# Values of the memory tokens with stationary weights, and another order of the first phase, in a two-part kernel that keeps TensorE busy

## The chip, the cores and the metric

The kernel runs on one core of one Trainium2 chip. The metric is device time in microseconds of one execution. Runs of this kernel agree within half a microsecond, so a difference of about 0.2% (2.5 us) can be told from no change.

The engines are named as the profile names them: PE is TensorE (PEld its weight loads), DVE is VectorE, ACT is ScalarE, POOL is GpSimd, and SP is SyncE, which here only issues DMAs. Each engine takes its instructions in order: one that waits holds up everything behind it on the same engine.

## The reference

Two independent computations on inputs of 2048 tokens with 1024 features, their results side by side:

```python
# Part A: a diagonal state space layer, states complex
dt = jnp.exp(log_dt); Lam_bar = jnp.exp(dt * Lam)
Bu = jnp.einsum('bld,pd->blp', x + 0j, B_bar)
for t in range(L):
    h = Lam_bar[None, :] * h + Bu[:, t, :]
y = 2.0 * jnp.einsum('blp,dp->bld', hseq, Cmat).real + x * Dskip
# Part B: attention in 64 segments of 32 tokens, 8 memory tokens in front of each, 32 heads of 128
for s in range(n_seg):
    h = jnp.concatenate([mem, xs], axis=1)
    q, k, v = (einsum('btd,dhe->bhte', h, W) for W in (Wq, Wk, Wv))
    p = _softmax(where(mask, q @ k * scale, -1e9))
    o = einsum('bhte,hed->btd', p @ v, Wo)
    mem = o[:, :M, :]          # the next segment's memory
    outs.append(o[:, M:, :])
out = jnp.concatenate([a, b], axis=-1)
```

## The kernel before

Part B's recurrence from segment to segment is replaced by a guess of the memory tokens that a last step compares with what comes out. The guess needs 73 columns (`NM`) for the memory tokens that are not ordinary tokens; they stand as columns 2048 to 2120 of `xe`, the transposed input, and are called `memT`.

**First phase (0 to 347 us).** PE alternates between two kinds of work. `values()` computes part B's values: `v_pair` makes two tiles of 128 tokens by 512 value columns, each by eight matmuls of 512 moving columns (`v_mm`, L411) into a PSUM buffer psP or psS (two of each, used in turn), ACT copies each tile to SBUF (L75, buffer `b_vst`), and `v_st` (L419) stores a pair to DRAM by SP's queue. The first eight pairs go to eight buffers of their own (`a_hs` in the profile); from the ninth pair on there are two `b_vst` buffers, so a pair's first copy needs the store of the pair two before to have landed. `stage1(pc, tb)` does part A: 32 times (8 blocks of states by 4 blocks of 512 tokens) 16 matmuls of 512 columns (L256) into psO (two buffers), then on DVE two products with the rotation table from psO (L263, L264), a difference and a sum in fp32 (L266, L267) and two scans along time (L270, L271). `post` then turns the scanned sums back: ACT rounds them to bf16 (`a_g`, one buffer, L288), and DVE makes two products and a sum (L290 to L292). `tables(pc)` makes the next block's rotation tables on DVE and ACT once in four stages. Three or four value tiles stand between two stages, and `og` (L468, 64 moving columns) now and then.

In the first phase the order in which instructions stand on an engine is the tile framework's, except where `keep_in_program_order` pins an instruction to where the program has it. Pinned are the matmuls of the beginning, the scans, all of `post`, the loads of part A's transposed input (`load_x`, `xT`, a transposing DMA of 1 MB each), the loads of Wv from head block 2 on, and the stores `v_st` of the beginning. `post` of stage n-1 is called half way through the value tiles that follow stage n.

**Second phase (347 to 465 us).** `stage2` multiplies the states by C (L310), `guess` makes the guessed memory.

**Attention (465 to 1017 us).** `proj` makes q and k of two heads at a time (L570, eight matmuls of 480 columns a group, and L553), `attention` does eleven units of scores, mask and values for each pair of heads (L596, L599, L603, L614, L619, L621). Values come from DRAM: `load_v(hp)` (L585, L586) reads a pair of heads from `vx` and `vt`. For each of the eight head blocks `v_mem(hb)` makes the values of the 73 memory columns: it loads Wv (1 MB, L403), takes `memT` as the stationary operand and 512 value columns of Wv as the moving one (L502, eight matmuls), copies 73 rows by 512 on ACT, and stores the rows by two DMAs (L505 into `vx`, L506 into `vt`). `v_mem(0)` stands behind nine groups of `proj`, `v_mem(hp + 1)` at unit 4 of pair hp.

**Output (1017 us to the end).** `op` multiplies by Wo (L670), `check` compares the guess (L715: 256 matmuls of 73 moving columns).

Of the kernel before, what the change touches and what calls it, by code (L numbers as in the profile page):

```python
# [9 lines left out]
BF16 = mybir.dt.bfloat16  # L10
I32 = mybir.dt.int32
ACT = mybir.ActivationFunctionType
ALU = mybir.AluOpType
# [13 lines left out]
HB = 8; HP = 16  # L27
# [7 lines left out]
NMX = 7  # L35
NM = NTL + NMX
# [97 lines left out]
class PartA:  # L134
# [92 lines left out]
    def load_x(self, tb):  # L227
        k = self.k
        self.xT[tb] = k.w8((KC, TB), "xT")
        k.tc.keep_in_program_order(  # L230
            k.SP.dma_start(self.xT[tb], self.x[0][tb * TB:(tb + 1) * TB, :], transpose=True))

    def load_b(self, pc):
        k = self.k
# [12 lines left out]
    def stage1(self, pc, tb):  # L247
        k = self.k; V, PE = k.V, k.PE
        pin = k.tc.keep_in_program_order
        if tb == 0:  # L250
            self.carry = None
        cs, rot, ed = self.tabs
        u = k.ps("O")
        for i in range(2):
            for c in range(KC):
                m = PE.matmul(u[:, i, :], self.bt[:, i, c, :], self.xT[tb][:, c, :], start=(c == 0), stop=(c == KC - 1))  # L256
                if self.pin:
                    pin(m)
        c_ = cs[:, 0, 0:TB].unsqueeze(1).to_broadcast([128, 2, TB])
        s_ = cs[:, 1, 0:TB].unsqueeze(1).to_broadcast([128, 2, TB])  # L260
        a = self.wp.tile([128, 2, TB], FP32, name="a_a")
        b = self.wp.tile([128, 2, TB], FP32, name="a_b", bufs=1)
        V.tensor_tensor(a[:], u[:], c_, ALU.mult)  # L263
        V.tensor_tensor(b[:], u[:], s_, ALU.mult)  # L264
        wr, wi = a[:, 0, :], a[:, 1, :]
        V.tensor_tensor(wi, wi, b[:, 0, :], ALU.subtract)  # L266
        V.tensor_tensor(wr, wr, b[:, 1, :], ALU.add)  # L267
        rb = self.rr[:, pc:pc + 1].to_broadcast([128, TB])
        ini = self.carry
        pin(V.tensor_tensor_scan(wr, rb, wr, 0.0 if ini is None else ini[:, 0:1], ALU.mult, ALU.add))  # L270
        pin(V.tensor_tensor_scan(wi, rb, wi, 0.0 if ini is None else ini[:, 1:2], ALU.mult, ALU.add))  # L271
        if tb < NB - 1:
            nx = self.wp.tile([128, 2], FP32, name="a_nx"); tt = self.wp.tile([128, 2], FP32, name="a_tt")
            V.tensor_scalar(tt[:], ed[:, 0:2], wi[:, TB - 1:TB], None, ALU.mult)
            V.scalar_tensor_tensor(nx[:], ed[:, 2:4], wr[:, TB - 1:TB], tt[:], ALU.mult, ALU.add)
            self.carry = nx
        if tb not in self.hs:
            self.hs[tb] = self.hsp.tile([128, PC, 2, TB], BF16, name="a_hs", bufs=4)
        self.prev, self.last = self.last, [a, rot, self.hs[tb][:, pc, :, :]]

    def post(self, last):
        if last is None:
            return
        k = self.k; V = k.V
        pin = k.tc.keep_in_program_order
        a, rot, hp = last
        g = self.wp.tile([128, 2, TB], BF16, name="a_g", bufs=1)
        pin(k.S.activation(g[:], a[:], ACT.Copy))  # L288
        n = self.wp.tile([128, 2, TB], BF16, name="a_n", bufs=1)
        pin(V.tensor_tensor(hp, g[:, 0:1, :].to_broadcast([128, 2, TB]), rot[:, 0:2, :], ALU.mult))  # L290
        pin(V.tensor_tensor(n[:], g[:, 1:2, :].to_broadcast([128, 2, TB]), rot[:, 1:3, :], ALU.mult))
        pin(V.tensor_tensor(hp, hp, n[:], ALU.add))  # L292

    def stage2(self, pool, dB):

# [21 lines left out]
class PartB:  # L317
    def __init__(self, k, x, mem0, Wq, Wk, Wv, Wo, out):
        self.k = k
        self.x, self.mem0, self.out = x, mem0, out  # L320
        self.Wf = [w.rearrange("(c p) h e -> p c (h e)", p=128) for w in (Wq, Wk, Wv)]
        self.Wo = Wo.rearrange("h e d -> e h d")
        self.vx = [k.drp.tile([NSLOT, 512], BF16, name=f"b_vx{i}") for i in range(HB)]
        self.vt = [k.drp.tile([NTL, 512], BF16, name=f"b_vt{i}") for i in range(HB)]
        self.os = [k.drp.tile([T, 1024], BF16, name=f"b_os{i}") for i in range(4)]
        self.omd = k.drp.tile([MT, H * E], BF16, name="b_omd")
        self.od = k.drp.tile([128, H * L], BF16, name="f_od")
        c = k.cst
        self.m0T = c.tile([128, KC, M], BF16, name="b_m0T")
        self.gm = c.tile([128, KC, NM], FP32, name="b_gm")  # L330
        self.xbar = c.tile([128, KC, NSEG], BF16, name="b_xbar")
        self.ogT = c.tile([128, H, NSEG], BF16, name="b_ogT")
        self.accE = c.tile([128, HP * NU], FP32, name="b_accE")
        self.rall = c.tile([128, HP * NU * 4], FP32, name="b_rall")
        self.flag = c.tile([1, 1], I32, name="b_flag")
# [62 lines left out]
    def load_wv(self, hb, w=None, parts=1, e=None, js=None):  # L398
        if w is None:
            w = self.k.w8((KC, 512), "wv")  # L400
        n = KC // parts
        for i in js or range(parts):
            d = (e or self.k.SP).dma_start(w[:, i * n:(i + 1) * n, :], self.Wf[2][:, i * n:(i + 1) * n, hb * 512:(hb + 1) * 512])  # L403
            if self.pin and hb > 1:
                self.k.tc.keep_in_program_order(d)
        return w


# [6 lines left out]
    def v_st(self, hb, q, st, e):  # L415
        vx = self.vx[hb]
        s0 = GX + 2 * q * 128
        n = 2 if q < 7 else 1
        d = e.dma_start(vx[s0:s0 + n * 128, :].rearrange("(i p) n -> p i n", p=128), st[:, 0:n, :])  # L419
        if self.pin:  # L420
            self.k.tc.keep_in_program_order(d)
        if q == 7:
            e.dma_start(vx[0:64, :], st[0:64, 1, :])
            e.dma_start(vx[T - 32:T + 32, :], st[64:128, 1, :])
# [70 lines left out]


    def v_mem(self, hb):
        k = self.k
        w = self.load_wv(hb)
        p = k.ps("P")  # L500
        for c in range(KC):
            k.PE.matmul(p[0:NM, :], self.memT[:, c, :], w[:, c, :], start=(c == 0), stop=(c == KC - 1))  # L502
        st = self.p3.tile([NM, 512], BF16, name="b_vmst", bufs=2)
        k.copy("s", st[:], p[0:NM, :])
        k.SP.dma_start(self.vx[hb][64:64 + NMX, :], st[0:NMX, :])  # L505
        k.SP.dma_start(self.vt[hb][:], st[NMX:NM, :])  # L506


    def qk_init(self, pool):
        V, G = self.k.V, self.k.G  # L510
        self.qk = []
        for i in range(2):
            pair = []
            for n in "qk":
                t = pool.tile([128, 2, QW], BF16, name=f"b_{n}{i}", bufs=1)
                V.memset(t[:, :, 64 + NMX:GX], 0.0)
                V.memset(t[:, :, 21 * GW + 64:21 * GW + GX], 0.0)
                V.memset(t[:, :, NG * GW:QW], 0.0)
                pair.append(t)
            self.qk.append(pair)  # L520
        self.vb, self.mb = [], []
        for i in range(2):
            t = pool.tile([GW, NG, VW], BF16, name=f"b_v{i}", bufs=1)
            G.memset(t[:, :, 0:1], 1.0)
            G.memset(t[:, :, VW - 1:VW], 1.0)
            self.vb.append(t)
        for i in range(4):
            t = pool.tile([GW, 4 * GW + 32], BF16, name=f"b_m{i}", bufs=1)
            G.memset(t[:, 4 * GW:4 * GW + 32], 0.0)
            self.mb.append(t)  # L530
# [315 lines left out]
def kernel_main(tc, A_x, A_Lre, A_Lim, A_Bre, A_Bim, A_Cre, A_Cim, A_logdt, A_Dskip, B_x, B_mem0, B_Wq, B_Wk, B_Wv, B_Wo, out,  # L846
                force=False, dbg=None):
    with ExitStack() as ctx:
        k = K(tc, ctx)
# [3 lines left out]
        a = PartA(k, A_x, A_Lre, A_Lim, A_Bre, A_Bim, A_Cre, A_Cim, A_logdt, A_Dskip, out)  # L853
        b = PartB(k, B_x, B_mem0, B_Wq, B_Wk, B_Wv, B_Wo, out)
# [10 lines left out]
        with pool("p1", "right") as p1:  # L865
# [54 lines left out]
            for n in range(PC * NB):  # L920
# [5 lines left out]
                if tb == 1 and pc + 1 < PC:  # L926
                    nbt = a.load_b(pc + 1)
                want = 20 + 4 * (n + 1) if n < 4 else 36 + (92 * (n - 3) + 27) // 28
                half = done + 2
                while done < want:  # L930
                    next(v, None); done += 1
                    if done == half:
                        a.post(a.prev)
                while done >= 32 and oged < done // 16:
                    b.og(oged, wvs.pop(oged))
                    oged += 1
# [15 lines left out]
                    a.load_c(0, 0)  # L952
                if n == 29:
                    a.load_c(0, 1)
            a.post(a.last)
            k.V.memset(b.rall[:], 0.0)
            a.load_c(1, 0)
            a.load_c(1, 1)
# [20 lines left out]
        with pool("p3", "right") as p3:  # L979
            b.p3 = p3  # L980
            b.qk_init(p3)
            pr, at = b.proj(), b.attention()
            for _ in range(9):
                next(pr)
            b.v_mem(0)
            for _ in range(9):
                next(pr)
            done = 18
            b.wo0, b.acc = [], {}
            early = b.op_some([(0, 0), (1, 0)], range(3), "P")  # L990
            for n, (hp, u) in enumerate(at):
                if u == 4 and hp < 7:
                    b.v_mem(hp + 1)
                if u == 4 and 8 <= hp < 12:
                    w = k.w8((8, 512), "wo0")
                    k.SP.dma_start(w, b.Wo[:, 8 * (hp - 8):8 * (hp - 7), 0:512])
# [113 lines left out]
```

## Time and profile before

| | |
|---|---|
| median of three runs | 1250.3 us (1250.12 to 1250.6) |
| the profiled execution, its own time | 1250.12 us |
| its span in the profile | 1248.4 us, so 1.7 us lie around it |
| PE busy | 1236.3 us, 99% of the span |
| DVE, ACT, POOL busy | 609.4, 329.3, 199.5 us |
| mean granted TensorE clock | 0.998 |

A row of the timeline gives start, duration, engine, line, operation, tiles and, in brackets, the engine's idle time before it and what ended that. Matmuls are pipelined, so a matmul's duration (379 ns for 512 columns) is longer than the time until the next one starts; what a group of matmuls costs is read from where the next group starts.

### The profile page before, as it was taken

The page shows a single profiled execution, that of the slowest core. Times are in us where ns is not written, and L with a number is a line of the kernel's source. Part 1 is how long each engine was busy: PE and PEld are TensorE (multiplying, and loading weights), DVE is VectorE, ACT ScalarE, POOL GpSimd, SP SyncE. Part 2 cuts the span into 40 slices and gives each one's busy share as a digit, 9 for nine tenths or more (in the row PEclk, how much of TensorE's full clock was granted, in tenths as well). Part 3 has the DMA queues.
Part 4 walks back from the last instruction along what each step waited for, and adds up shares of the span by engine and source line. Part 5 has one row for each costly group of instructions (what it writes and reads, how often), then busy time and mean ns, then how long its engine had stood idle before and what let it go on. Part 6 is the DMA issues. An engine that isn't in the chain of part 4 may idle for free. (4 is left out here: it accounts for less than half of the span.)

```text
span 1248.4 us, 19205 instructions
## 1 busy us (share of the span) xinstructions
PE 1236.3 (99%) x7852; PEld 651.9 (52%) x7923; DVE 609.4 (49%) x1117; ACT 329.3 (26%) x757; POOL 199.5 (16%) x284
## 2 busy tenths in 40 slices
PE   9999999999999999999999999999999999999998
PEld 4444444444455445555555655555556554454443
DVE  4889999999931122444444444444444450011000
ACT  4444434444210002323333333333233320000000
POOL 2000000000032130222222222322232230000000
PEclk9999999999999999999999999999999999999999
DMA  9932232333666557576767544645575469606000
GB/s 238 261 109 68 89 98 71 91 93 85 151 213 201 138 163 139 96 141 141 142 122 156 114 122 94 129 82 94 105 139 105 72 195 217 159 18 152 17 26 19
DMA packets 296995, 151.81 MB, mean 122 GB/s; under 512 B 138440, under 2 KB 290240, under 8 KB 296904
## 3 DMA queue, kind: packets, MB, share of 16 engines
q1 hardware_dynamic: 295640, 149.11, 51.9%
q8 instruction: 63, 1.03, 0.4%
q10 hardware_dynamic: 1264, 1.44, 0.4%
q14 instruction: 28, 0.23, 0.1%
HBM read 73.70 MB, written 43.66 MB: 94 GB/s over the span
## 5 line engine op out<-in xcount | busy, mean ns | idle before, releaser
L570 PE MATMUL psP<-b_xe,w 128*128 128x480 bf16 x2048 | 439.7, 366 | 0.0
L570 PEld LDWEIGHTS <-w 128*128 128x128 bf16 x2048 | 194.2, 98 | 185.2
L603 POOL TENSOR_TENSOR b_m<-b_e,maskB 99x396 bf16<-99x396 bf16 x160 | 139.2, 871 | 356.3 <-ACT b_e L599 356.3
L77 DVE CAST b_q<-psP 128x480 bf16<-128x480 f32 (+1 forms) x192 | 98.2, 533 | 150.9 <-PE psP L570 139.4
L411 PEld LDWEIGHTS <-b_xe 128*128 128x128 bf16 x1024 | 99.9, 98 | 120.4 <-ACT b_xe L75 0.6
L670 PEld LDWEIGHTS <-b_ol 128*128 128x128 bf16 x1024 | 99.5, 98 | 117.5
L75 ACT ACTIVATE b_k<-psP 128x480 bf16<-128x480 f32 x128 | 73.1, 571 | 314.3 <-PE psP L570 314.3
L599 ACT ACTIVATE b_e<-psS 99x396 bf16<-99x396 f32 x176 | 87.4, 496 | 173.8 <-PE psS L596 166.6
L621 DVE TENSOR_TENSOR b_ot<-psO,b_rall 99x512 bf16<-99x512 f32 x176 | 121.7, 692 | 6.4
L256 PE MATMUL psO<-w,a_bt 128*128 128x512 bf16 x496 | 114.8, 379 | 0.8
L670 PE MATMUL psS<-w,b_ol 128*128 128x512 bf16 x438 | 99.0, 379 | 0.6
L619 DVE RECIPROCAL b_rall<-psO 99x4 f32<-99x4 f32 x176 | 31.2, 177 | 136.3 <-PE psO L614 136.2
L411 PE MATMUL psS<-w,b_xe 128*128 128x512 bf16 x378 | 90.1, 379 | 0.4
L411 PE MATMUL psP<-w,b_xe 128*128 128x512 bf16 x376 | 89.8, 379 | 0.4
L256 PEld LDWEIGHTS <-a_bt 128*128 128x128 bf16 x512 | 49.7, 98 | 59.0
L310 PEld LDWEIGHTS <-a_hs 128*128 128x128 bf16 x512 | 49.5, 98 | 58.3
L614 PE MATMUL psO<-b_v,b_m 99*128 99x129 bf16 x704 | 70.5, 221 | 0.1
L77 DVE CAST b_ost<-psS 128x512 bf16<-128x512 f32 x13 | 9.0, 692 | 125.4 <-PE psS L670 112.3
L596 PEld LDWEIGHTS <-b_k 128*128 128x128 bf16 x704 | 49.8, 98 | 33.4 <-issue 0.5
L596 PE MATMUL psS<-b_q,b_k 128*128 128x99 bf16 x704 | 60.1, 208 | 0.2
L75 ACT ACTIVATE b_vst<-psS 128x512 bf16<-128x512 f32 x56 | 33.4, 597 | 98.1 <-PE psS L411 70.2
L310 PE MATMUL psS<-w,a_hs 128*128 128x512 bf16 x245 | 57.3, 380 | 0.6
(201 smaller groups left out, 1084.0 us busy)
## 6 DMA issues: line engine op xcount, KB each, us to landing
b_v<-b_vx SPq DMA_DIRECT2D x16, 1056.0 KB
b_os<-b_ot SPq DMA_DIRECT2D x16, 960.0 KB
w<-in_B_Wv_dram SPq DMA_DIRECT2D x14, 1024.0 KB
b_vx<-b_vst SPq DMA_DIRECT2D x48, 256.0 KB
w<-in_B_Wo_dram SPq DMA_DIRECT2D x12, 1024.0 KB
w<-in_B_Wq_dram SPq DMA_DIRECT2D x16, 512.0 KB
w<-in_B_Wk_dram SPq DMA_DIRECT2D x16, 512.0 KB
a_xn<-in_A_x_dram SPq DMA_DIRECT2D x32, 128.0 KB
```

Source lines behind the costliest of these rows:

```text
L75: self.S.activation(out, in_, ACT.Copy)
L77: self.V.tensor_copy(out, in_)
L256: m = PE.matmul(u[:, i, :], self.bt[:, i, c, :], self.xT[tb][:, c, :], start=(c == 0), stop=(c == KC - 1))
L310: PE.matmul(py[:], self.hs[tb][:, pc, i, tt * 128:(tt + 1) * 128], self.ct[half, i][:, pc, :], start=(pc == 0 and i == 0), stop=(pc == PC ...
L411: m = self.k.PE.matmul(p[:], self.xe[:, c, t * 128:(t + 1) * 128], w[:, c, :], start=(c == 0), stop=(c == KC - 1))
L570: PE.matmul(p[:, 0:480], w[:, i * KC + c, hh * 128:(hh + 1) * 128], self.xe[:, c, 480 * q:480 * q + 480], start=(c == 0), stop=(c == KC - 1))
L596: PE.matmul(s[:, j * GW:(j + 1) * GW], kt[:, hh, g0:g0 + 128], qt[:, hh, g0:g0 + GW], start=True, stop=True)
L599: k.S.activation(e[:], s[0:GW, 0:4 * GW], ACT.Exp, scale=float(E) ** -0.5, accum_out=self.accE[0:GW, i:i + 1])
L603: k.G.tensor_tensor(v4(m[:, 0:4 * GW]), v4(e[:]), mask[0:GW, :, :].unsqueeze(2).to_broadcast([GW, 2, 2, GW]), ALU.mult)
L614: PE.matmul(o[:, gg, cs], m[:, j * GW:j * GW + 128], vt[:, 2 * u + gg, cs], start=True, stop=True)
L621: V.tensor_tensor(ot[:, 2 * u:2 * u + 2, :].rearrange("p g (h e) -> p g h e", h=2), oa[:, :, 1:257].rearrange("p g (h e) -> p g h e", h=2) ...
L670: k.PE.matmul(self.acc[t, half], ol[:, h8, tt * 128:(tt + 1) * 128], self.wo_half(half, h), start=(h == 0), stop=(h == H - 1))
```

## The change

In `v_mem` the operands change places. For each of the four heads of a block, and each of the eight chunks of features, a 128 by 128 piece of Wv is the stationary operand and the 73 columns of `memT` are the moving one. The result has value features on the partitions and memory tokens along the row. ACT copies it to one of two buffers of 128 columns a head, whose columns 73 to 127 were set to zero once; one DMA writes it to a scratch `vm` of 512 by 128 in DRAM; a transposing DMA reads the scratch back as rows; and two DMAs store the rows as before. These four DMAs are pinned in SP's order, and `v_mem` is now a generator: the program calls it at units 3, 5 and 7 of a pair of heads, and for head block 0 behind the third, seventh and eleventh group of `proj`.

In the first phase `load_x`, the loads of Wv and `v_st` are no longer pinned. The difference of L266 is issued on POOL. `post` is split: `round`, the rounding on ACT, stands right behind the next stage's matmuls and is pinned; `post`, the DVE part, stands behind the next stage's scans, and only its first product is pinned.

```diff
     def load_x(self, tb):
-        k.tc.keep_in_program_order(
-            k.SP.dma_start(self.xT[tb], ..., transpose=True))
+        k.SP.dma_start(self.xT[tb], ..., transpose=True)
     def stage1(self, pc, tb):
...
+        self.round()
...
-        V.tensor_tensor(wi, wi, b[:, 0, :], ALU.subtract)
+        k.G.tensor_tensor(wi, wi, b[:, 0, :], ALU.subtract)
         V.tensor_tensor(wr, wr, b[:, 1, :], ALU.add)
...
+        self.post()
...
-        self.prev, self.last = self.last, [a, rot, self.hs[tb][:, pc, :, :]]
+        self.last = [a, rot, self.hs[tb][:, pc, :, :]]
-    def post(self, last):
...
-        pin(k.S.activation(g[:], a[:], ACT.Copy))
...
-        pin(V.tensor_tensor(hp, g[:, 0:1, :]..., rot[:, 0:2, :], ALU.mult))
-        pin(V.tensor_tensor(n[:], g[:, 1:2, :]..., rot[:, 1:3, :], ALU.mult))
-        pin(V.tensor_tensor(hp, hp, n[:], ALU.add))
+    def round(self):
+        if self.last is not None:
+            g = self.wp.tile([128, 2, TB], BF16, name="a_g", bufs=1)
+            k.tc.keep_in_program_order(k.S.activation(g[:], self.last[0][:], ACT.Copy))
+            self.last[0] = g
+    def post(self):
...
+        self.k.tc.keep_in_program_order(
+            V.tensor_tensor(hp, g[:, 0:1, :]..., rot[:, 0:2, :], ALU.mult))
+        V.tensor_tensor(n[:], g[:, 1:2, :]..., rot[:, 1:3, :], ALU.mult)
+        V.tensor_tensor(hp, hp, n[:], ALU.add)
     def load_wv(self, hb, w=None, parts=1, e=None, js=None):
-            d = (e or self.k.SP).dma_start(...)
-            if self.pin and hb > 1:
-                self.k.tc.keep_in_program_order(d)
+            (e or self.k.SP).dma_start(...)
     def v_st(self, hb, q, st, e):
-        d = e.dma_start(vx[s0:s0 + n * 128, :]..., st[:, 0:n, :])
-        if self.pin:
-            self.k.tc.keep_in_program_order(d)
+        e.dma_start(vx[s0:s0 + n * 128, :]..., st[:, 0:n, :])
     def v_mem(self, hb):
         w = self.load_wv(hb)
         p = k.ps("P")
-        for c in range(KC):
-            k.PE.matmul(p[0:NM, :], self.memT[:, c, :], w[:, c, :], start=(c == 0), stop=(c == KC - 1))
-        st = self.p3.tile([NM, 512], BF16, name="b_vmst", bufs=2)
-        k.copy("s", st[:], p[0:NM, :])
-        k.SP.dma_start(self.vx[hb][64:64 + NMX, :], st[0:NMX, :])
-        k.SP.dma_start(self.vt[hb][:], st[NMX:NM, :])
+        for h in range(4):
+            for c in range(KC):
+                k.PE.matmul(p[:, h * NM:(h + 1) * NM], w[:, c, h * 128:(h + 1) * 128], self.memT[:, c, :],
+                            start=(c == 0), stop=(c == KC - 1))
+        st = self.vmst[hb % 2]
+        k.copy("s", st[:, :, 0:NM], p[:, 0:4 * NM].rearrange("p (h n) -> p h n", h=4))
+        pin(k.SP.dma_start(self.vm[hb].rearrange("(h p) n -> p h n", p=128), st[:]))
+        yield
+        vr = self.p3.tile([128, 512], BF16, name="b_vmr", bufs=1)
+        pin(k.SP.dma_start(vr[:], self.vm[hb][:, :], transpose=True))
+        yield
+        pin(k.SP.dma_start(self.vx[hb][64:64 + NMX, :], vr[0:NMX, :]))
+        pin(k.SP.dma_start(self.vt[hb][:], vr[NMX:NM, :]))
+        yield
 # kernel_main, first phase: the call of post half way through the value tiles goes
-                    if done == half:
-                        a.post(a.prev)
-            a.post(a.last)
+            a.round()
+            a.post()
 # kernel_main, attention
-            for _ in range(9):
+            vm = b.v_mem(0)
+            for i in range(18):
                 next(pr)
-            b.v_mem(0)
-            for _ in range(9):
-                next(pr)
+                if i in (2, 6, 10):
+                    next(vm)
-                if u == 4 and hp < 7:
-                    b.v_mem(hp + 1)
+                if u == 3 and hp < 7:
+                    vm = b.v_mem(hp + 1)
+                if u in (3, 5, 7) and hp < 7:
+                    next(vm)
```

More of the change, by code (lines that the diff above doesn't have):

```diff
@@ L229, in load_x @@
         self.xT[tb] = k.w8((KC, TB), "xT")
-        k.tc.keep_in_program_order(
-            k.SP.dma_start(self.xT[tb], self.x[0][tb * TB:(tb + 1) * TB, :], transpose=True))
+        k.SP.dma_start(self.xT[tb], self.x[0][tb * TB:(tb + 1) * TB, :], transpose=True)
     def load_b(self, pc):
@@ L276, in stage1 @@
             self.carry = nx
+        self.post()
         if tb not in self.hs:
             self.hs[tb] = self.hsp.tile([128, PC, 2, TB], BF16, name="a_hs", bufs=4)
-        self.prev, self.last = self.last, [a, rot, self.hs[tb][:, pc, :, :]]
-    def post(self, last):
-        if last is None:
-            return
[L284 to L287, printed above, removed]
-        pin(k.S.activation(g[:], a[:], ACT.Copy))
+        self.last = [a, rot, self.hs[tb][:, pc, :, :]]
+    def round(self):
+        if self.last is not None:
+            k = self.k
+            g = self.wp.tile([128, 2, TB], BF16, name="a_g", bufs=1)
+            k.tc.keep_in_program_order(k.S.activation(g[:], self.last[0][:], ACT.Copy))
+            self.last[0] = g
+    def post(self):
+        if self.last is None:
+            return
+        V = self.k.V
+        g, rot, hp = self.last
+        self.last = None
         n = self.wp.tile([128, 2, TB], BF16, name="a_n", bufs=1)
-        pin(V.tensor_tensor(hp, g[:, 0:1, :].to_broadcast([128, 2, TB]), rot[:, 0:2, :], ALU.mult))
-        pin(V.tensor_tensor(n[:], g[:, 1:2, :].to_broadcast([128, 2, TB]), rot[:, 1:3, :], ALU.mult))
-        pin(V.tensor_tensor(hp, hp, n[:], ALU.add))
+        self.k.tc.keep_in_program_order(
+            V.tensor_tensor(hp, g[:, 0:1, :].to_broadcast([128, 2, TB]), rot[:, 0:2, :], ALU.mult))
+        V.tensor_tensor(n[:], g[:, 1:2, :].to_broadcast([128, 2, TB]), rot[:, 1:3, :], ALU.mult)
+        V.tensor_tensor(hp, hp, n[:], ALU.add)
     def stage2(self, pool, dB):
@@ L323, in __init__ @@
         self.vx = [k.drp.tile([NSLOT, 512], BF16, name=f"b_vx{i}") for i in range(HB)]
+        self.vm = [k.drp.tile([512, 128], BF16, name=f"b_vm{i}") for i in range(HB)]
         self.vt = [k.drp.tile([NTL, 512], BF16, name=f"b_vt{i}") for i in range(HB)]
@@ L402, in load_wv @@
         for i in js or range(parts):
-            d = (e or self.k.SP).dma_start(w[:, i * n:(i + 1) * n, :], self.Wf[2][:, i * n:(i + 1) * n, hb * 512:(hb + 1) * 512])
-            if self.pin and hb > 1:
-                self.k.tc.keep_in_program_order(d)
+            (e or self.k.SP).dma_start(w[:, i * n:(i + 1) * n, :], self.Wf[2][:, i * n:(i + 1) * n, hb * 512:(hb + 1) * 512])
         return w
@@ L418, in v_st @@
         n = 2 if q < 7 else 1
-        d = e.dma_start(vx[s0:s0 + n * 128, :].rearrange("(i p) n -> p i n", p=128), st[:, 0:n, :])
-        if self.pin:
-            self.k.tc.keep_in_program_order(d)
+        e.dma_start(vx[s0:s0 + n * 128, :].rearrange("(i p) n -> p i n", p=128), st[:, 0:n, :])
         if q == 7:
@@ L498, in v_mem @@
         k = self.k
+        pin = k.tc.keep_in_program_order
         w = self.load_wv(hb)
         p = k.ps("P")
-        for c in range(KC):
-            k.PE.matmul(p[0:NM, :], self.memT[:, c, :], w[:, c, :], start=(c == 0), stop=(c == KC - 1))
-        st = self.p3.tile([NM, 512], BF16, name="b_vmst", bufs=2)
-        k.copy("s", st[:], p[0:NM, :])
-        k.SP.dma_start(self.vx[hb][64:64 + NMX, :], st[0:NMX, :])
-        k.SP.dma_start(self.vt[hb][:], st[NMX:NM, :])
+        for h in range(4):
[12 more added lines that the diff above has]
+        yield
     def qk_init(self, pool):
@@ L520, in qk_init @@
             self.qk.append(pair)
+        self.vmst = []
+        for i in range(2):
+            t = pool.tile([128, 4, 128], BF16, name=f"b_vmst{i}", bufs=1)
+            V.memset(t[:, :, NM:128], 0.0)
+            self.vmst.append(t)
         self.vb, self.mb = [], []
@@ L928, in kernel_main @@
                 want = 20 + 4 * (n + 1) if n < 4 else 36 + (92 * (n - 3) + 27) // 28
-                half = done + 2
                 while done < want:
                     next(v, None); done += 1
-                    if done == half:
-                        a.post(a.prev)
                 while done >= 32 and oged < done // 16:
```

## The prediction

> **What bounds the kernel now.** First the table of windows over the first phase, for all engines (busy us, instructions in brackets, then clock, DMA share, GB/s):
>
> ```profile
> 100.00:150.00 50.00, 49.74 (x257) 23.15 (x260) 48.23 (x64) 20.26 (x34) 0.00 (x0) 1.00 0.27 79
> 250.00:300.00 50.00, 49.74 (x256) 23.16 (x260) 47.69 (x63) 20.65 (x34) 0.00 (x0) 1.00 0.27 79
> ```
>
> PE (the first number after the comma) is full and DVE (the third) nearly: 96% and 95%. The page says PE 99% over the whole span, and the starts of the matmuls agree: 512 columns start 216 ns apart and 480 columns 202 ns, with no gap of note between 20 us and 1014 us. So every us taken off PE's own work is a us of time, every new wait of PE is a us lost, and DVE has about 2 us of room in 50.
>
> Then PE's timeline at the two lines that price the new matmuls, and at the old ones (time is read from start to start):
>
> ```profile
> 479.29 1.89 PE L502 MATMUL psP<-w,b_xe 128*73 128x512 bf16 x8
> 481.02 11.51 PE L570 MATMUL psP<-b_xe,w 128*128 128x480 bf16 x56
> ...
> 1081.26 2.32 PE L715 MATMUL psP<-c_om,w 128*128 128x73 bf16 x64
> 1083.42 6.85 PE L670 MATMUL psS<-w,b_ol 128*128 128x512 bf16 x30
> ```
>
> Old group: 1.73 us. 64 matmuls of 73 columns with new weights each: 2.16 us, so 32 take 1.08.
>
> Last, ACT's timeline, where the first phase has its tightest place:
>
> ```profile
> 52.85 0.60 ACT L75 ACTIVATE b_vst<-psP 128x512 bf16<-128x512 f32 x1 [1.08 <-PE psP L411]
> 59.87 0.60 ACT L75 ACTIVATE b_vst<-psS 128x512 bf16<-128x512 f32 x1 [6.42 <-DMA b_vx<-b_vst]
> 60.36 0.59 ACT L75 ACTIVATE b_vst<-psP 128x512 bf16<-128x512 f32 x1
> ```
>
> ACT had to wait for a store before it could empty a value tile. PE lost nothing: the four PSUM buffers covered it.
>
> **Part 1, `v_mem` on PE.** 8 blocks x (1.73 - 1.08) = 5.2 us less. Bounds: by the 64-column row of L468 (32 matmuls in 0.93 us) 6.4; by the 128-column transposes of L377 (56 ns apart, 1.79 us) nothing. 73 columns is the exact row, so 5.2. The copy shrinks from 512 to 292 columns and two memsets join DVE where it is half idle: nothing.
>
> **Part 1, DMAs.** `v_mem(0)` moves from behind nine groups of `proj` to behind three. Its Wv load is issued at 464.69, when stage 2's last matmul frees the buffer, and lands 5.6 us later by the trace's semaphore updates; three groups take 3 x 1.62 = 4.9. PE waits 0.8 us, once, and everything behind it in order with it. The detour (write, transposing read, rows) adds about 7 us on SP: the write lands behind the next 1 MB of Wv (4.9 us for L505 there), a small transposing load takes 3.5 us (the rows of L237), the row stores 2 to 3. Queued behind on SP are the loads of `b_v`, Wq and Wk. For block 0, starting 9.7 us earlier pays for it: values loads go out at about 483 instead of 486.75, and the first L614 is at 501.78. Later blocks need theirs some 30 us later; the Wq load behind waits for a buffer anyway. So 0; had the values come 3 us later than before, PE would lose 1.5.
>
> **Part 2, DMA order.** In the built order of the changed kernel SP's queue is the same up to the third store; then the transposing loads xT1, xT2, xT3 and Wv blocks 2 and 3 come ahead of store 9, which before stood ahead of xT1. In the trace a DMA behind a full queue lands after the one ahead by 3.6 us (xT behind stores: 45.01 to 48.62, 60.21 to 63.82), 4.1 (Wv: 63.82 to 67.82) or 0.8 (stores of 256 KB); an xT alone takes 6.5 from issue (29.26 to 35.73). From 34.34, when SP is free: xT1 40.8, stores 4 and 5 42.4, xT2 46.5, store 6 47.3, Wv2 51.4, store 7 52.2, xT3 55.8, store 8 56.6, Wv3 60.7, store 9 61.5. Cross-check: Wv3 landed at 67.82 with 2 us of L237 loads and four stores ahead that now stand behind. Store 9 frees the `b_vst` buffer of tile 21, copied at 47.72 before; now its copy ends at 62.2. Tile 25 takes the same psS buffer and started at 56.10. Four buffers no longer cover it: PE waits 6.2 us, and nothing later gives it back. Bounds: 4.8 (all stores at 0.5, Wv at 3.9) and 7.5 (1.1 and 4.3).
>
> **Part 2, the difference on POOL.** DVE's timeline of one stage:
>
> ```profile
> 67.80 1.21 DVE L264 TENSOR_TENSOR a_b<-psO,a_cs 128x1024 f32<-128x1024 f32 x1
> 69.05 0.69 DVE L266 TENSOR_TENSOR a_a<-a_a,a_b 128x512 f32<-128x512 f32 x1
> 69.66 0.68 DVE L267 TENSOR_TENSOR a_a<-a_a,a_b 128x512 f32<-128x512 f32 x1
> 70.38 1.29 DVE L270 TENSOR_TENSOR_SCAN a_a<-a_rr,a_nx,a_a 128x512 f32<-128x512 f32 x1
> ```
>
> DVE is spared 0.61 us a stage (L266 to L267); the nearest row on POOL is `a_xd`, 128x512, 1.15 us. It ends before the second scan, which needs it, if the two engines run side by side: gain for DVE, none for PE. The other new wait: the second product is pulled ahead to right behind the sum, where it needs the rounding of its own stage; the one `a_g` buffer is free only after the first product, ACT takes 1.05, DVE fills 0.6: 0.45 us idle in stages without table work. Together -0.2 a stage. Nothing for PE.
>
> If they cannot run side by side, the difference stands in DVE's line: +1.15 - 0.61 + 0.45, a plain stage of 8.7 us (L263 to L292) becomes 9.7. Four stages with 2.7 us of tables, 0.9 of which fill the idle gaps, and 0.4 without a carry: 40.2 us, against PE's 38.8 (75.23 to 346.74 is 28 stages). DVE falls behind by 1.4 in four stages, 9.8 over seven blocks, plus hand-overs of some 0.06 twice a stage: 3.4. ACT passes it on: `round` stands ahead of the copies of the next tiles. About 6 of the 13 are absorbed by psO's two buffers and the copies' slack; PE loses 7. Bounds 0 and 13.
>
> Which? L603 on POOL takes 869 to 875 ns whether or not DVE's L621 runs beside it, but L621 and L312 read one operand from PSUM. No row has POOL beside a DVE operation with both operands in SBUF, as the sum, the scans and the products have. The one place with both engines on SBUF data speaks for turns:
>
> ```profile
> 2.21 0.11 POOL L104 MEMSET maskA<- 32x32 bf16 x1
> ...
> 2.41 0.29 POOL L104 MEMSET maskA<- 32x32 bf16 x1
> 2.47 0.24 POOL L107 MEMSET maskA<- 32x1 bf16 x1
> 2.77 0.12 POOL L104 MEMSET maskA<- 32x32 bf16 x1
> ```
>
> DVE's CAST of L190 runs from 1.99 to 2.64; the two stretched memsets both end at 2.71, 0.06 behind it. I take turns as likelier.
>
> [...]
>
> **Sum.** The profiled execution took 1250.1 (0.2 under the median). -5.2 + 0.8 + 6.2 = +1.8, 1252 with the engines side by side; +7 with turns: 1259.
>
> **Rivals.** (a) Side by side: 1252.0 (1250.5 to 1253.5). For it: POOL's rows beside L621. (b) Faster: the early stores do not hold PE. One mechanism: if the queues do not land strictly in order, store 9, issued by 55.4, lands 2.5 later (store 1: 25.40 to 27.90), before 58; then tile 21's copy ends at 58.5, PE waits 2.4 and the sum is 1250.1 - 5.2 + 0.8 + 2.4 = 1248.1; with none left, 1245.7. The gain wins if store 9 lands before 59.8 (a wait under 5.2 - 0.8 = 4.4) and (a) holds. Against: in the trace landings follow issue order throughout 25 to 69 us. (c) Worse turns: hand-overs of 0.3 us a stage more pass on another 8: 1267. (d) The narrow matmuls are held by their weight loads (98 ns busy each): the 5.2 vanish, 1264 with turns; L715 has the same loads and speaks against it.
>
> **How the numbers follow.** Turns 0.60; (a) 0.25; (b) 0.07; (c) and (d) 0.08. A difference under 0.2% (2.5 us) cannot be told from none. Faster: (b), 0.06. Same: of (a) two thirds (up to 1252.8) and a little of (b), 0.17. Slower: the rest, 0.77. The range reaches from the low half of (a), 1250.8, to (c), 1267.
>
> **What would show it.** PE: eight groups of 32 matmuls, each 1.08 us to the next start; one wait of 5 to 7 us near 56 to 63 us, put down to ACT, ACT there to a store's DMA; 0.8 us before the first `v_mem`. Turns: the sum or the first scan on DVE starts 1.2 us late or POOL's 32 differences last far over 1.15; PE waits for ACT's copies after 200 us and at the start of stage 2, 7 us in all. Wrong if PE's first phase ends as early as before, if POOL's differences last 1.15 with DVE's scans going on beside them, or if PE idles in the attention.

## The result, and the profile after

The changed kernel takes 1257.24 us (median of four runs, 1256.65 to 1258.17), the kernel before 1250.44 beside it: a ratio of 1.0055 [1.0038, 1.0073], 6.8 us slower. The prediction said 1259.0 (1250.8 to 1267) and slower. The profiled execution took 1258.17 us with a span of 1256.5, 8.1 more than before. Runs of one kernel spread more than the first three did: the 28 runs of the kernel before that stand beside experiments 5 to 7 lie between 1249.71 and 1252.29. Differences of 1 to 2 us are therefore read from rows of the traces.

First the steady part. The windows that were shown of before, in the kernel after:

```profile
100.00:150.00 50.00, 49.74 (x256) 23.18 (x260) 47.63 (x59) 20.52 (x33) 8.41 (x5) 1.00 0.27 80
250.00:300.00 50.00, 49.69 (x255) 23.19 (x260) 48.40 (x58) 17.89 (x31) 8.40 (x5) 1.00 0.26 74
```

PE is as full as it was (49.74 and 49.69 of 50); POOL (8.41) is new, and DVE has not become less busy, although 32 of its operations moved to POOL. So the loss is not spread over the phase. PE's list of waits (engine, line, what it waited for: us in total, times, longest) says where it is:

```profile
PE psS L418 <- ACT b_vst L75: 8.7, 1, 8.7
PE psO L911 <- DVE a_hs L908: 1.3, 1, 1.3
PE psS L318 <- ACT b_vst L75: 1.2, 1, 1.2
```

The 1.3 of L911 stood in the kernel before too. New are one wait of 8.7 us and one of 1.2. PE's timeline around the long one:

```profile
52.93 3.62 PE L255 MATMUL psO<-w,a_bt 128*128 128x512 bf16 x15
65.21 3.57 PE L418 MATMUL psS<-a_hs,b_xe 128*128 128x512 bf16 x8 [8.66 <-ACT b_vst L75]
68.58 3.19 PE L418 MATMUL psP<-a_hs,b_xe 128*128 128x512 bf16 x8
71.61 1.89 PE L418 MATMUL psS<-a_hs,b_xe 128*128 128x512 bf16 x8
```

And ACT's, which answers to the three rows of before at 52.85 to 60.36:

```profile
64.56 0.60 ACT L75 ACTIVATE b_vst<-psS 128x512 bf16<-128x512 f32 x1 [21.19 <-DMA b_vx<-b_vst]
65.06 0.59 ACT L75 ACTIVATE b_vst<-psP 128x512 bf16<-128x512 f32 x1
66.12 0.60 ACT L75 ACTIVATE b_vst<-psS 128x512 bf16<-128x512 f32 x1 [0.47 <-DMA b_vx<-b_vst]
```

PE finished the second stage of part A and found all four PSUM buffers full; ACT sat idle for 21 us, the last 17 of them with a full buffer in front of it, until store 9 had landed. That is the mechanism that the prediction named. But look at the starts after the wait: a group of eight matmuls takes 3.37 and 3.03 us (65.21 to 68.58 to 71.61) where it takes 1.72 elsewhere (71.61 to the next start, 73.33). The windows give the reason in the column before the last two, the granted clock:

```profile
60.00:65.00 5.00, 0.00 (x0) 0.00 (x0) 0.00 (x0) 0.44 (x1) 0.00 (x0) 0.60 1.20 238
65.00:70.00 5.00, 4.79 (x12) 1.71 (x12) 1.82 (x3) 3.27 (x6) 0.00 (x0) 0.50 0.62 183
70.00:75.00 5.00, 5.00 (x22) 2.10 (x21) 4.93 (x5) 1.19 (x2) 1.77 (x1) 0.88 0.15 52
```

The clock fell to half while PE idled and stayed there for 6.0 us of work. By the trace's record of the clock it was half from 60.96 to 71.20; work of 3.0 us at full clock took 6.0. This cost, 3.0 us, has no term in the prediction.

The new matmuls of `v_mem`:

```profile
483.02 1.24 PE L510 MATMUL psP<-b_xe,w 128*128 128x73 bf16 x32
484.10 16.16 PE L590 MATMUL psP<-b_xe,w 128*128 128x480 bf16 x79
```

1.08 us to the next start, as predicted, and no wait ahead of them. Last, DVE and POOL in a stage, beside the four rows of before from 67.80 on:

```profile
104.27 0.69 DVE L267 TENSOR_TENSOR a_a<-a_a,a_b 128x512 f32<-128x512 f32 x1
104.38 1.71 POOL L266 TENSOR_TENSOR a_a<-a_a,a_b 128x512 f32<-128x512 f32 x1 [8.51 <-DVE a_b L264]
104.99 2.17 DVE L270 TENSOR_TENSOR_SCAN a_a<-a_rr,a_a 128x512 f32<-128x512 f32 x1
...
110.59 0.69 DVE L299 TENSOR_TENSOR a_n<-a_g,a_rot 128x1024 bf16<-128x1024 bf16 x1 [0.46 <-ACT a_g L287]
```

POOL's difference takes 1.71 where `a_xd` alone took 1.15, and the first scan beside it 2.17 where it took 1.29. In about one stage of four POOL starts first, and then DVE's sum is the one that is stretched: at 133.46 it takes 1.76 instead of 0.69. So in these rows the two engines took turns, in part. The last row has the 0.46 us in which the second product waits for its own stage's rounding (0.45 predicted).

Added up from the profile: 8.7 for the wait, 3.0 for the half clock, 1.4 at the start of stage 2 (a wait of 1.24; with the difference back on DVE, experiment 4, the starts on its two sides move apart by 1.40), less 5.2 for `v_mem`: +7.9, against 8.1 in the span.

### The profile page after: what moved, and what is told of

Same layout as the page of the kernel before. It is cut to its first block, busy times and chain, and to the rows that moved or that the text cites. A ratio compares the mean times of both kernels' runs of the same rounds, so it can differ in the third digit from the quotient of the medians.

```text
span 1256.5 us, 19677 instructions
## 1 busy us (share of the span) xinstructions
PE 1234.8 (98%) x8044; PEld 654.3 (52%) x8115; DVE 620.8 (49%) x1087; ACT 326.4 (26%) x757; POOL 253.6 (20%) x316
## 4 chain that ended last, share of the span: by engine, by line
PE 77%; DVE 18%; ACT 1%; SPq 1%; issue 1%; DMA 1%; POOL 0%; ACTq 0%
PE psP L590 33%; PE psS L690 10%; PE psP L690 5%; PE psP L318 4%; PE psS L318 4%; DVE a_a L270 4%; PE psP L573 4%; PE psO L634 3%; PE psP L418 2%; PE psS L616 2%; PE psS L418 2%; DVE a_a L271 2%; DVE a_b L264 2%; DVE a_a L263 2%; PE psO L690 2%; DVE a_a L267 2%
## 5 line engine op out<-in xcount | busy, mean ns | idle before, releaser
L266 POOL TENSOR_TENSOR a_a<-a_a,a_b 128x512 f32<-128x512 f32 x32 | 54.1, 1689 | 299.1 <-DVE a_b L264 267.1
L287 ACT ACTIVATE a_g<-a_a 128x1024 bf16<-128x1024 f32 x32 | 33.8, 1055 | 108.5 <-DVE a_hs L298 108.5
```

## The experiments

The theory after the result, called theory 1 in the expectations: the change's loss is the order of SP's queue in the first 60 us, with the half clock that follows from PE's idling; `v_mem` is a gain of 5.2; POOL's difference and the split of `post` cost little. The main rival is the prediction's own sum, with 7 us for turns.

**1. `v_mem` alone.** The kernel before with the `v_mem` hunks of the change, and nothing of the first phase:

```diff
+        for h in range(4):
+            for c in range(KC):
+                k.PE.matmul(p[:, h * NM:(h + 1) * NM], w[:, c, h * 128:(h + 1) * 128], self.memT[:, c, :], ...)
 # with the scratch vm, the generator and its calls; load_x, load_wv, v_st, stage1 and post as before
```

> The kernel before with only the v_mem part of the change (narrow moving operand, padded scratch in DRAM, transposing read, calls at other units); the first phase is that of before. Theory 1 (the group of matmuls is 0.65 us cheaper, the DMAs lie beside other work): eight groups of 1.08 instead of 1.73 us, 5.2 us less, 1250.4 - 5.2 = 1245.2 us, and no wait of PE in the attention. The prediction's own step adds a wait of 0.8 us for the first Wv: 1246.0. Rival (the detour through DRAM makes the values late somewhere, as the first phase of the changed kernel may hide by being late itself): PE waits for values in the first pair of heads and the time is over 1247.

Measured: 1244.78 us (1244.49 to 1245.38, five runs), ratio 0.9955 [0.9942, 0.9969], so 5.6 us faster. No wait of PE in the attention, and none for the first Wv: `v_mem(0)`'s group starts at 469.76, the next at 470.85. Theory 1 holds, and the prediction's 0.8 does not come. The detour through DRAM is hidden. This version is faster than both kernels.

**2. The queue's order put back.**

```diff
-        k.SP.dma_start(self.xT[tb], ..., transpose=True)
+        k.tc.keep_in_program_order(k.SP.dma_start(self.xT[tb], ..., transpose=True))
 # and the pins of load_wv and v_st
```

> The changed kernel with the three pins on SP's queue put back (loads of xT, of Wv, stores of values); all else as changed. Theory 1 (the loss is the order of the queue: a wait of 8.7 us at 56.6 us, and 3.0 us more because the granted clock drops to half behind it): 1257.2 - 8.7 - 3.0 = 1245.5 us, no wait over 1 us before 80 us, clock full from 20 us on. The prediction's terms (wait of 6.2 and no clock term; turns of POOL and DVE cost 7): 1257.2 - 6.2 = 1251.0. Rival (the half clock comes from something else than the idle time, such as the load of DMAs there): the half clock stays and the time is about 1248.5.

Measured: 1246.64 us (1246.14 to 1248.28), ratio 0.9970 [0.9958, 0.9982]. 10.6 us came back (11.3 between the spans of the two profiled executions, 1256.5 and 1245.2), where 11.7 were expected: more than the wait of 8.7, and the clock is 1.00 in all windows from 50 to 80 us. So wait and half clock go together with the order, and the prediction's 6.2 alone is refuted. Which of the three pins is the one that matters was not run apart. What is left against experiment 1 is 1.9 us; PE's starts in the two traces are the same until stage 2 and 1.42 us apart from there on, behind this row of the list of waits:

```profile
PE psS L319 <- ACT b_vst L75: 1.2, 1, 1.2
```

**3. The queue's order alone.** The kernel before without the three pins:

```diff
-        k.tc.keep_in_program_order(k.SP.dma_start(self.xT[tb], ..., transpose=True))
+        k.SP.dma_start(self.xT[tb], ..., transpose=True)
 # and without the pins of load_wv and v_st
```

> The kernel before without the three pins on SP's queue; nothing else changed (the order of all other engines is that of before). Theory 1: the same wait of about 8.7 us and the half clock behind it, 1250.4 + 8.7 + 3.0 = 1262.1 us. The prediction's term of 6.2 us alone: 1256.6. Rival (the half clock in the changed kernel has to do with POOL or with the moved rounding, not with the wait): a wait of 8.7 us with full clock behind it, 1259.1.

Measured: 1261.46 us (1259.17 to 1262.13), ratio 1.0084 [1.0071, 1.0098]: 11.1 us slower, with a wait of 8.3 at 56 us and half clock for the 5.4 us of work behind it, which costs 2.7. The other engines' order is that of before, so neither POOL nor the moved rounding is needed. The single parts add up: -5.6 (experiment 1) + 11.1 + 1.9 (2 against 1) = +7.4, measured +6.8.

**4. The difference back on DVE.**

```diff
-        k.G.tensor_tensor(wi, wi, b[:, 0, :], ALU.subtract)
+        V.tensor_tensor(wi, wi, b[:, 0, :], ALU.subtract)
```

> The changed kernel with the difference of L266 back on DVE; all else as changed. Theory 1 (taking turns makes DVE late by 1.4 us only, at the end of the first phase): 1257.2 - 1.4 = 1255.8 us or a little more, since the second product's wait for its own stage's rounding stays. The prediction's term for turns, 7 us: 1250.2. Rival (POOL's difference does no harm at all): 1257.2.

Measured: 1254.62 us (1253.53 to 1255.81), ratio 1.0031 [1.0019, 1.0044], 2.6 less than the changed kernel. The wait at the start of stage 2 is gone: between two starts on its two sides the traces move apart by 1.40 us. The rest is not POOL's: the first phase's wait was 9.2 in this trace, but the half clock ended 4.0 us after PE's restart instead of 6.0, 1.0 us less lost. So turns cost 1.4, not 7. The runs of this kernel fall into two groups, near 1253.6 and 1255.6, which another phase of the clock's steps would give (the last section tells of them). That is not shown: the mean granted clock of the three faster runs is 0.996 to 0.997, that of the three slower ones 0.994 to 0.996.

**5. POOL alone, and the split alone.** On the kernel before, first

```diff
-        V.tensor_tensor(wi, wi, b[:, 0, :], ALU.subtract)
+        k.G.tensor_tensor(wi, wi, b[:, 0, :], ALU.subtract)
```

> The kernel before with only the difference of L266 on POOL. Theory 1 (POOL and DVE take turns in part: the scan beside it is 0.9 us longer and DVE is spared 0.6, so a plain stage of 8.7 us becomes 9.0, still under PE's 9.7): PE waits nowhere for it and the time is that of before, 1250.3 us. Rival A (POOL's difference alone makes the copies late at the start of stage 2 as in the changed kernel): 1.4 us more, 1251.7. Rival B (the prediction's turns, 1.15 us a stage and hand-overs): 7 us more, 1257.

then

```diff
-                    if done == half:
-                        a.post(a.prev)
 # round() behind stage1's matmuls and post() behind its scans, as in the change
```

> The kernel before with only the split of post (rounding right behind the next stage's matmuls, the DVE part behind its scans, as in the changed kernel). Theory 1 (DVE idles 0.46 us in a stage for the rounding, a plain stage of 9.2 us stays under PE's 9.7): 1250.3 us, no wait at the start of stage 2. Rival (the split makes DVE and ACT late and POOL is not needed for it): 1.4 us more, 1251.7.

Measured: 1250.27 us (1249.67 to 1252.02, 11 runs), ratio 0.9998 [0.9989, 1.0007], and 1250.50 us (1250.16 to 1251.15, 11 runs), ratio 0.9997 [0.9988, 1.0006]. Neither does anything by itself, and neither has a wait at stage 2; together they cost the 1.4. The last stage of the first phase shows why. PE's last 16 matmuls and DVE's first product of them, first with POOL alone, then in experiment 2, where both parts are in:

```profile
336.74 3.62 PE L256 MATMUL psO<-w,a_bt 128*128 128x512 bf16 x16
341.03 1.22 DVE L263 TENSOR_TENSOR a_a<-psO,a_cs 128x1024 f32<-128x1024 f32 x1
```

```profile
337.41 3.62 PE L256 MATMUL psO<-w,a_bt 128*128 128x512 bf16 x16
348.45 1.22 DVE L264 TENSOR_TENSOR a_a<-psO,a_cs 128x1024 f32<-128x1024 f32 x1
```

From start to start 4.29 us and 11.04. The kernel before has 3.66 here and the split alone 4.83. So DVE is late by 0.6, by 1.2, and with both by 7.4. PE's stages take 9.36 us on the average (75.47 to 337.41 is 28 stages in experiment 2), DVE's with both parts 9.59 (its first products at 79.97 and 348.45), so that the lateness piles up. With either part alone DVE still catches up: at the 23rd stage its first product comes 3.7 us (POOL alone) and 3.8 us (split alone) behind PE's start, as in the kernel before (3.7).

**6. PE kept busy during the wait.**

```diff
                 a.stage1(pc, tb)
+                if n == 1:
+                    pw = k.ps("O")
+                    for i in range(35):
+                        tc.keep_in_program_order(k.PE.matmul(pw[:, i % 2, :], b.xe[:, 0, 0:128], b.xe[:, 0, 0:512], start=True, stop=True))
```

> The changed kernel with 35 matmuls of 512 columns into a free psO buffer, right behind the second stage of part A, where PE otherwise waits 8.7 us; nobody reads what they write. Theory 1 (the granted clock drops because PE idles there): they fill 7.6 us of the wait, the clock stays full, the first value tile starts at the same time (about 65.2 us of the span) and the next three groups take 1.73 us instead of 3.37, 3.03 and 1.73: 2.0 to 3.0 us less than the changed kernel, 1254.2 to 1255.2. Rival (the slow matmuls come from the DMAs beside them or from the wait itself): half clock and 1257.2 as before.

Measured: 1255.57 us (1253.84 to 1256.11), ratio 1.0034 [1.0021, 1.0046], a little above the expected 1254.2 to 1255.2; 1.7 us under the changed kernel by the medians, 2.6 by the two ratios, whose intervals overlap. All six runs lie below all four of the changed kernel, and the clock settles it. The windows that had 0.60 and 0.50:

```profile
60.00:65.00 5.00, 3.72 (x18) 1.57 (x16) 0.00 (x0) 0.35 (x1) 0.00 (x0) 1.00 1.28 167
65.00:70.00 5.00, 4.65 (x21) 2.15 (x22) 1.76 (x3) 3.85 (x7) 0.00 (x0) 1.00 0.63 188
```

The clock is full, with the same DMAs beside it (DMA share 1.28 and 0.63, after 1.20 and 0.62), and the first three value groups start 1.73 us apart. They begin at 65.30 (65.21 in the changed kernel), and the third begins at 68.75 instead of 71.61: 2.9 earlier, about the 3.0 that the half clock cost. So the half clock comes from PE's idling, not from the DMAs. Useless matmuls made the kernel faster.

**7. The stores on another queue.**

```diff
-                    yield from b.v_pair(hb, q, wvs[hb], k.SP)
+                    yield from b.v_pair(hb, q, wvs[hb], nc.scalar if 3 <= q < 6 else k.SP)
```

> The changed kernel with the stores of the 7th to the 12th pair of value tiles issued by ACT instead of SP; the loads of xT and Wv stay ahead on SP's queue. Theory 1a (the store is late because it stands in SP's queue behind the loads): store 9 lands within about 3 us of its issue, before 56 us, PE does not wait there, the clock stays full, and what is left is the 1.4 us of the start of stage 2: 1257.2 - 8.7 - 2 to 3 = 1245.5 to 1246.6 us. Theory 1b (the DMA engines themselves are full of the loads and serve in order of issue, whichever queue it was): store 9 lands only with the loads issued before it and the time stays near 1257.

Measured: 1248.13 us (1246.72 to 1250.52, 11 runs), ratio 0.9978 [0.9969, 0.9987]: most of the loss is gone, but neither 1a nor 1b is quite right. Store 9 was issued at 45.59 and landed at 51.91 by the semaphore updates (56.63 and 64.45 in the changed kernel), so standing behind the loads in SP's queue was most of its delay; but it took 6.3 us and landed together with xT2 (52.08), where the first stores took 2.5 to 3. PE still waits 1.0 in the first phase. ACT's timeline shows why:

```profile
54.97 0.37 ACTq L426 DMA_DIRECT2D b_vx<-b_vst  x1
55.44 0.60 ACT L75 ACTIVATE b_vst<-psS 128x512 bf16<-128x512 f32 x1 [8.35 <-DMA w<-in_B_Wv_dram]
60.08 0.60 ACT L75 ACTIVATE b_vst<-psS 128x512 bf16<-128x512 f32 x1 [3.56 <-DMA b_vx<-b_vst]
```

ACT issued the store after store 9 only at 54.97, 7.9 us after its copy. Just before, ACT waits for a semaphore that a Wv load of SP's queue uses too; that load was issued at 47.65 and landed at 54.90. So on ACT, too, a store of this kernel stood behind one of the loads, with ACT's copies behind it. This store landed at 60.00, and PE's wait ended with the copy that it let go.

Here DVE is late by more, the wait at stage 2 is 2.1, and in the profiled execution the clock fell there too (windows around it):

```profile
348.00:350.00 2.00, 0.07 (x3) 0.00 (x0) 1.51 (x3) 1.42 (x2) 0.00 (x0) 1.00 0.00 0
350.00:352.00 2.00, 1.61 (x5) 0.75 (x6) 2.00 (x3) 1.37 (x4) 0.00 (x0) 0.65 0.46 163
352.00:354.00 2.00, 2.00 (x6) 0.65 (x5) 1.93 (x3) 0.00 (x0) 1.23 (x1) 0.50 0.47 128
```

The profiled execution is the slowest of the eleven. The four runs with a mean granted clock of 0.997 or 0.998 took 1248.65 us or more; of the seven with 0.999 or 1.000 six took 1248.13 or less, so the clock probably did not fall in most of them.

**8. Shorter fillers.** As experiment 6, one execution each:

```diff
-                    for i in range(35):
+                    for i in range(29):     # the second kernel: 24
```

> The changed kernel with 29 matmuls (6.3 us) instead of 35 in the wait, which leaves PE idle for about 3 us. In the traces so far the granted clock changes only on a grid of 3.413 us that starts when it first becomes full. Theory 1 (the clock drops at the end of a grid interval in which PE ran for less than about half): the idle time lies in one or two intervals; if one of them holds over about 2 us of it, the clock is half for the intervals after it, otherwise it stays full. Rival (only an interval without any matmul lowers it): full clock, since 3 us cannot fill an interval.

> The same with 24 matmuls (5.2 us), which leaves PE idle for about 4 us. Theory 1: at least one interval of the grid holds 2 us of it or more, so the clock drops to half in the run. Rival (only an interval without any matmul): it drops only if a whole interval falls into the 4 us, about one time in six.

Measured: 1255.35 and 1256.85 us. With 29 PE waited only 0.6 us, since its own work reached this place 1.9 us later in this run (57.86 against 56.01 in experiment 6) and the store did not land later: it tells nothing. With 24 PE waited 4.1 us, and the clock fell for one interval (0.66 in this window), although no interval of the grid was without matmuls, so the rival is out:

```profile
65.00:70.00 5.00, 4.63 (x14) 1.76 (x14) 1.67 (x2) 3.33 (x6) 0.00 (x0) 0.66 0.64 194
```

## Why the prediction came out, point by point

The mechanisms were mostly right, but that the total came out so near is luck, because errors of both signs cancelled: +2.5 in the wait, +3.0 for the clock, -5.6 for turns, -0.8 for the first Wv. Together -0.9 from 1259.0 is 1258.1, the profiled execution's 1258.17.

- `v_mem` on PE, -5.2: right. Groups of 1.08; alone -5.6 (5.4 in the span, 0.3 of it a short wait at the start that is in the trace of before and not in this one). The rival of weight loads that hold the narrow matmuls is out.
- `v_mem(0)`'s wait for Wv, +0.8: it did not come, because the wrong load was taken for it. The load issued at 464.69 in the trace of before is that of `v_mem(1)`. `v_mem(0)`'s went out at 436.06 there; after, it was issued at 449.88 and landed at 456.57, 26 us ahead of its matmuls at 483.02, while the load at 478.14 lands from 483.19 on, too late to be theirs.
- The DMAs of `v_mem`, 0: right, by experiment 1.
- The DMA order, +6.2: right in kind, mis-sized, 8.7 (8.3 to 9.2 in three traces). The sum put store 9's landing at 61.5; it landed at 64.45. The row that failed is the transposing load behind a full queue: xT2 landed 5.4 us after the store ahead of it (42.85 to 48.22) and xT3 4.6 (53.73 to 58.37), where 4.1 and 3.6 were used, and the second Wv took 4.9 (58.73 to 63.67) instead of 4.1. The stores' 0.8 and less were right but for one that took 1.4 (41.44 to 42.85). PE came to the place 0.45 later than in the trace of before (56.55 for 56.10), so 2.95 at the store became 2.5 of wait. The upper bound, 7.5, was too low for the same reason.
- The clock, no term: wrong. The prediction took a wait of 6 us as a wait of 6 us; PE ran at half speed for 6.0 us after it. Experiments 3 and 6 show that it comes with the wait and from PE's idling. 3.0 us was a third of the wait's own cost.
- Turns, +7: the mechanism is there, the size was not. Of the stage's +0.99, the scan's part is 0.89 instead of 1.15 (2.09 to the next scan's start after 1.20 before), and the 0.06 for hand-overs twice a stage are not seen on top: DVE's plain stage is 9.37 us (the starts of L263 at 350.93 and 360.30) instead of 9.7. PE's side was miscounted as well: 75.23 to 346.74 is 29 stages, not 28, so PE takes 37.4 us for four and not 38.8. With 37.4 the prediction's own 40.2 would have made DVE late by 20, not 9.8, over seven blocks; that the two errors offset each other is luck too. DVE ended 7.4 us late instead of 13.2. That 6 of it would be absorbed was right: 7.4 less 1.4. Small errors in two periods that are near each other became a factor of five in the end. Where DVE's sum was first, POOL started 0.11 behind it and took 0.56 more than `a_xd` alone, about the 0.58 that was left of the sum; the scan took 0.88 more, less than the 1.10 that was left of POOL's operation. How much of it reached PE was decided by the slack of the stage: nothing with POOL alone (experiment 5), 1.4 with the split.
- Rival (a), side by side, is out by 1.71 and 2.17; (b) by store 9 at 64.45; (c) by 1.4.

## What to carry to other kernels

Price a wait of the bound engine with what follows it: here 8.7 us of idling brought 3.0 more. Where one change bundles several, price and run each by itself; here the gain of one part was buried under the queue order of another, and `v_mem` alone is the version to keep. Where an engine's period is a few per cent under that of the bound engine, two small delays that are free alone can pile up together (here DVE took 9.59 us a stage with both against PE's 9.36, and 1.4 us were lost), so add them before calling either of them free.

## What the runs showed of the hardware that was not expected

In the traces the granted clock changed only on a grid. The stretches between its changes were multiples of 3.413 us: in the changed kernel 54.613 of full clock (16 intervals), 10.240 of half (3) and 1184.425 of full again (347), in the kernel before 1239.038 of full (363); the half stretch that the end of a trace cuts off is left aside. The windows of the others agree: half for 10.3 and 10.2 us in experiments 4 and 3, for 3.4 in experiment 7 and in experiment 8 with 24 fillers. The grid is counted from where the clock first became full, at 6.35 us in the changed kernel and at 5.51 in the kernel before. PE's busy time in each interval, worked out from the matmuls of each trace: in the first phase and at stage 2 the clock fell at the end of intervals with 0 (the changed kernel and experiment 3), 0.42 (experiment 4), 1.26 (experiment 8, 24 fillers) and 1.31 us (experiment 7), and not of those with 1.50 (experiment 8, 24 fillers) and 1.78 (experiment 6). The last matmuls of the traces agree: it fell behind intervals with 0.29 (experiment 6), 0.97 (experiment 7) and 1.35 us (the kernel before), and not behind those with 1.56 (experiment 4), 1.85 and 1.94 (experiment 8) and 1.96 (the changed kernel). So the limit lay between 1.35 and 1.50 us here, 40% and 44% of an interval, each bound from one run. It came back at the end of an interval with 3.19 (experiment 7) or 3.41 us (the changed kernel), and not of those with 2.03 (experiment 3) and 2.58 (the changed kernel). That is why similar waits cost 2.0, 2.7 or 3.0 us in three traces. It is not the only reason for runs of one kernel to differ: the six of experiment 6, all with a mean granted clock of 0.999 or 1.000, still spread over 2.3 us.

One short wait was enough: in experiment 7 a wait of 2.1 us that fell whole into one interval was followed by an interval at half clock, about 1.6 us lost.

A store issued on another queue did not pass freely by the transposing loads: in experiment 7 it took 6.3 us beside them (45.59 to 51.91), and a store on SP's queue later in the same trace 2.1 without them (67.76 to 69.88).
